# Gated mix of sliding-window attention and a GELU MLP: 256-column products read their moving operand from two halves in turn, and a product and a store stand later in the order

## The chip, the cores and the metric

The kernel runs on one core of one Trainium2 chip. The metric is the device time of one execution in microseconds (us); lower is better. The engines are named as the profile names them: PE does matrix products, PEld the weight loads that overlap them, DVE is the vector engine, ACT the scalar (activation) engine, POOL the third elementwise engine, and SP issues the DMA transfers. Each engine works through its own list of instructions strictly in the order in which the program has them.

## The reference

One sequence of 2048 rows with 512 columns, float32. What is computed, cut to what matters:

```python
def _A_ref(x, wqkv, wo):            # H = 32 heads of 16, window W = 256
    q, k, v = split(x @ wqkv)
    scores = einsum("bhqd,bhkd->bhqk", q, k) * (16 ** -0.5)
    mask = (i - j >= 0) & (i - j < 256)
    p = softmax(where(mask, scores, -1e9))
    return einsum("bhqk,bhkd->bhqd", p, v) @ wo

def _B_ref(x, w1, b1, w2, b2):      # F = 1792
    return gelu(x @ w1 + b1) @ w2 + b2

g = sigmoid((x * gate_w).sum(-1, keepdims=True))
out = g * _A_ref(x, wqkv, wo) + (1 - g) * _B_ref(x, w1, b1, w2, b2)
```

## The kernel before

**Products in three parts.** Every float32 operand of a dense product is split into a high part (rounded to the type that PE multiplies in one pass) and a low part (the rest), and a product is the sum of high x high, high x low and low x high. `mm3` issues these three matmuls. The moving operand (the one that streams through PE, up to 512 columns) can be read straight through or "from its two halves in turn": column 0, column 256, column 1, column 257 and so on. `two` makes that view, and `pairs` is a view of the accumulator with the same order of columns. With both the result lies straight in the accumulator's addresses as streamed, so its reader has to take every second element: `sorted_` gives the first-half columns, then the second-half ones. Before the change, `mm3` does this only for 512 columns.

**Stages.** The 2048 rows are four tiles of T = 512, numbered t = 0 to 3. (1) `qkv(t)` transposes x on PE and makes q, k, v. For t = 0 it begins while the inputs still arrive: the first two q/k products, into accumulators `p[0]` and `p[1]`, are made in column halves of 256 by `qk_half` (48 matmuls, read straight through). `qk_out` then splits each accumulator: ACT copies the high part (`hi`), DVE subtracts the low part (`lo`). (2) Attention runs in 8 groups of 4 heads over 16 key blocks: `att_max` (product `sm`, then a maximum on DVE), `att_exp` (product `st`, exponential on ACT, mask on POOL), `att_pvs` (product with v, once per 512 rows). Its results, numerators and denominators, are added to a tile `nd` on DVE and stored to DRAM as `ND`. (3) Between the attention steps stand the products of the MLP (`mlp`: `u` is the first layer, `gelu` its activation on ACT and DVE, `y` the second layer). (4) `final(t)` loads the normalised attention output `ot` (tiles `ot_0` to `ot_3`, one per 128 columns), splits it into high and low (`hi` on ACT, `lo` on DVE), multiplies by wo into accumulators `a`, and DVE combines with the gate (`ev`, tile `ao`) before the result goes out. There are two accumulators of tag `d`, shared by all dense products. The very last row block is done in two pieces of 256 output columns (LASTN = 2), 24 matmuls, read straight through.

**Normalisation** of the attention output is `att_norm(t, c)`, where t is the row tile and c the quarter of the columns. It works through DRAM: load the denominators into `den`; `rcp` inverts them on DVE; `keep` stores them to `RD`; `back` loads the numerators `num` and the inverses `rb`, the latter spread over 16 rows; `mul` multiplies them on DVE (tile `num`); `store` writes `OT`. `load_part` later reads `OT` into `ot`.

**What sets the order.** The program is written out by a planner with a clock of its own, `now`, in planned nanoseconds. `after(ns, fn)` puts a step on a list with a due time; `tick(ns)` advances the clock by the planned cost of a piece of PE work and writes out all steps that have come due. `fill(ns)` takes dense work until its planned cost is used up, so the attention loop and the dense work are interleaved by planned cost. A `mm3` costs 681 planned ns (MM3), a `qk_half` 119 ns per matmul. DIVS holds the five delays of `att_norm`'s steps (rcp, keep, back, mul, store) from its start: the first row for c = 0 to 2, the second for c = 3. `load_part` asks every 500 planned ns whether its piece of OT is due.

Of the kernel before, what the change touches and what calls it, by code (L numbers as in the profile page):

```python
# [18 lines left out]
T = 512  # L19
NT = S // T  # L20
NB = T // 128
NC = D // 128
# [10 lines left out]
def gated_mix(ctx: ExitStack, tc: tile.TileContext, x, wqkv, wo, w1, b1, w2, b2, gate_w, out):  # L33
# [12 lines left out]
    def f32(ap):  # L46
        return ap.bitcast(F32)
# [60 lines left out]
    def two(v):  # L108

        return v.rearrange("p (a c) -> p c a", a=2)  # L110

    def halves(v):

        return v.rearrange("p (a c) -> p a c", a=2)

    def pairs(p):

        return p.rearrange("p (c a) -> p c a", a=2)
# [3 lines left out]
        return p.rearrange("p (c a) -> p a c", a=2)  # L122

    def mm3(p, lh, ll, rh, rl, first, last):
        if p.shape[1] == T:
            p, rh, rl = pairs(p), two(rh), two(rl)
        nc.tensor.matmul(p, lh, rh, start=first, stop=False)  # L127
        nc.tensor.matmul(p, lh, rl, start=False, stop=False)  # L128
        nc.tensor.matmul(p, ll, rh, start=False, stop=last)  # L129
# [193 lines left out]
    def qk_half(p, j, n, parts):  # L323

        w, xt = wt["qk", j], xts[0]
        h = slice(n * T // 2, (n + 1) * T // 2)
        for a, b in parts:
            for c in range(NC):
                nc.tensor.matmul(p[:, h], w[:, a, c], xt[:, c, b, h], start=(a, b, c) == (0, 0, 0),
                                 stop=(a, b, c) == (1, 0, NC - 1))  # L330
        return len(parts) * NC * 119

    def qk_out(t, j, p):

        i = j % NC
        dst = (SQ, SK)[j // NC][t][i // 2]
        e = sb.tile([128, 2, T], F32R, tag="h", bufs=7, name=f"qke{t}_{j}")

        h = 1 if j < NC else 0

        def hi():
            nc.scalar.activation(halves(e[:, h]), p, AF.Copy)  # L342

        def lo():
            nc.vector.tensor_sub(halves(e[:, 1 - h]), p, halves(f32(e[:, h])))  # L345

        def store():
            to = dst[:, :, :, i % 2].rearrange("h d s c -> (h d) s c")
            nc.sync.dma_start(to[:, 0:2], f32(e))
            if i < 2:  # L350
                nc.sync.dma_start(to[:, 2], f32(e[:, h]))
            else:
                twice.append((t, j, to[:, 2], to[:, h]))
            done.add(("qk", t, j))
        after(100, hi), after(700, lo), after(700 + HOLDQ, store)
# [37 lines left out]
    def qkv(t):  # L393
        last = t == NT - 1
        qk = [("qk", j) for i in range(NC) for j in (i, i + NC)]
        vs = [("v", b) for b in range(NB)]
        pieces = qk[:4] + vs + qk[4:] if last else qk + vs
        if t == 0:
            keys = qk + [("v", c) for c in range(NC)]
            load_xr(0, (0, 1))  # L400
            load_raw(keys[0], True)
            load_xr(0, (2, 3))
            for key in keys[1:]:
                load_raw(key, True)
            nc.sync.dma_start(gwb, gate_w.partition_broadcast(128))
            warm(WARM[0])
            qkv_x(0, 0), qkv_x(0, 1)
            split_now(keys[0], nc.gpsimd.tensor_copy, nc.vector)
            tables()
            warm(WARM[1])  # L410
            p = [ps.tile([128, T], F32, tag="d", bufs=2, name=f"qk0_{n}") for n in range(2)]
            j0, j1 = keys[0][1], keys[1][1]
            yield qk_half(p[0], j0, 0, [(0, 0)])
            qkv_x(0, 2)
            yield qk_half(p[0], j0, 0, [(0, 1), (1, 0)])
            split_now(keys[1], lambda o, i: nc.scalar.activation(o, i, AF.Copy), nc.vector)
            qkv_x(0, 3)
            parts = [(0, 0), (0, 1), (1, 0)]
            yield qk_half(p[1], j1, 0, parts)
            split(keys[2], nc.gpsimd)  # L420
            yield qk_half(p[0], j0, 1, parts)
            qk_out(0, j0, halves(p[0]))
            yield qk_half(p[1], j1, 1, parts)
            qk_out(0, j1, halves(p[1]))
        need(*[("x", t, b) for b in range(NB)])
        for n, (kind, j) in enumerate(pieces):
            if not last and XAT <= n < XAT + NC:
                nc.sync.dma_start(XT[t][n - XAT], f32(xts[t][:, n - XAT]))
            if kind == "qk":
                need(("w", (kind, j)))  # L430
            else:
                need(*[("w", ("v", c)) for c in range(NC)])
            if t == 0 and n == 10:
                nc.sync.dma_start(b1c, b1.rearrange("(f p) -> p f", p=128))
            if t == 0 and n < 2:
                pass
            elif kind == "qk":
                yield from qkv_qk(t, j)
            else:
                yield from qkv_v(t, j)  # L440
            if t == 1 and n % 3 == 2:
                clear_k(n // 3)
            if t == 2 and n < 4:
                clear_q(n)
            if t == 2 and n in (1, 2):
                load_kd(0, n - 1)
            if t == 2 and n in (8, 9):
                load_qd(0, n - 8)
            if t == 0:
                for i in ([3], [4], [5], [6], [7], [8], [9, 10], [11])[n] if n < 8 else []:  # L450
                    split(keys[i], nc.vector if i % 2 else nc.gpsimd)
                if n == 1:
                    after(4000, gate, 0)
                    after(4000, load_xr, 1)
            elif n == 0 and not last:
                load_xr(t + 1)
            if last and n not in (6, 7):
                load(later.pop(0))
            if last and n == len(pieces) - 1:
                for _ in range(4):  # L460
                    load(later.pop(0))
            xat = (5, 7, 8, 9) if t == 0 else (4, 6, 8, 10)
            if not last and n in xat:
                qkv_x(t + 1, xat.index(n))
            if not last and n == xat[-1] + 1:
                gate(t + 1)
# [422 lines left out]
    def final(t):  # L889
        if t == 0:  # L890
            load_o(1)
        ot = xts["o", t]
        parts = {}

        def begin(b, k, n):

            if b == 2 and t < 2:
                load_o(t + 2, range(NC - t))
            if b == 1 and t == 2:
                load_o(NT - 1, range(NC - 1, NC))  # L900
            if k == 0:
                parts[b] = half_pt(f"ao{t * NB + b}")
                after(0, scale_y, t * NB + b, parts[b])
            parts[b, k] = ps.tile([128, D // n], F32, tag="d", bufs=2, name=f"a{t}_{b}_{k}")

        def end(b, k, cs):
            nb, a, p = t * NB + b, parts[b], parts[b, k]

            def ev():
                need(("yb", nb))  # L910
                v = halves(a[:, cs])
                nc.vector.scalar_tensor_tensor(v, (sorted_ if p.shape[1] == T else halves)(p), g[:, nb:nb + 1], v,
                                               op0=ALU.mult, op1=ALU.add)

            def store():
                nc.sync.dma_start(out[nb * 128:(nb + 1) * 128, cs], a[:, cs])
            after(100, ev), after(100 + (HOLDO if nb < NT * NB - 2 else 800), store)

        turns = [(b, c) for b in range(NB) for c in range(NC)]
        if t == NT - 1:  # L920
            turns[:2 * NC] = [(b, c) for h in (range(NC - 1), [NC - 1]) for b in (0, 1) for c in h]
        for b, c in turns:
            n = LASTN if t * NB + b == NT * NB - 1 else 1
            for k in range(n):
                if n > 1:
                    if c:
                        continue
                    row = range(NC)
                else:
                    row = [c]  # L930
                cs = slice(k * D // n, (k + 1) * D // n)
                if c == 0:
                    begin(b, k, n)
                for e in row:
                    need(("w", ("wo", e)), ("ot", t, e))
                    w, ts = wt["wo", e], slice(b * 128, (b + 1) * 128)
                    mm3(parts[b, k], ot[e][:, 0, ts], ot[e][:, 1, ts], w[:, 0, cs], w[:, 1, cs], e == 0, e == NC - 1)
                    yield MM3 / n
                if row[-1] == NC - 1:
                    end(b, k, cs)  # L940
# [105 lines left out]
HOLD = 4000.0  # L1046
HOLDQ = 1500.0
HOLDO = 3000.0
DIVS = ((8000, 10000, 16000, 23000, 25000), (4500, 5700, 8500, 17000, 18500))
REST = 1000.0  # L1050
MXAT = 5500.0
AHEAD = 9e3
# [27 lines left out]
```

## Time and profile before

| | us |
|---|---|
| median of 3 runs | 713.68 (712.69 to 714.38) |
| the profiled execution | 713.22 |
| its span, first to last instruction | 711.4 |
| around the span (difference) | 1.82 |

Busy time and share of the span are given for each engine at the head of the profile; PE's matmuls are pipelined and overlap one another, so its busy time says where it had nothing at all to do, not how fast it went. How fast it went is read from the distance between the starts of neighbouring matmuls in the timeline. The "waits" view lists who waited for whom with the total, the number of times and the longest; the "chain" is the work that ended last, followed back from the end; "windows" gives the busy time of each engine in a stretch of the span. The granted TensorE clock was 1.00 through the run. The groups of instructions that cost most, by engine:

| engine | busiest group | busy us | instructions |
|---|---|---|---|
| PE | `sm` and `st` products of the attention | 295.8 | 1024 |
| DVE | maximum over the scores (`sm`, L555) | 232.8 | 512 |
| POOL | mask of the exponentials (`pt`, L611) | 215.1 | 538 |
| ACT | exponential (`pt`, L617) | 195.4 | 512 |

### The profile page before, as it was taken

How to read it: one execution, taken by the hardware profiler on the slowest of the kernel's cores; microseconds unless marked ns; L12 is line 12 of the kernel's file. 1: busy time of each engine (PE TensorE's matmuls, PEld its weight loads, DVE VectorE, ACT ScalarE, POOL GpSimd, SP SyncE). 2: the span in 40 equal slices, each digit the busy share in tenths (PEclk: the TensorE clock that was granted, in tenths of full speed). 3: DMA queues.
4: the chain of work that ended last, by engine and by line, in shares of the span. 5: the costliest groups of instructions: out<-in, count | busy, mean ns of one | idle time of the engine just before them, and what ended most of it. 6: DMA issues, size and time to landing. Idle time of an engine off the chain costs nothing.

```text
span 711.4 us, 17481 instructions
## 1 busy us (share of the span) xinstructions
PE 694.0 (98%) x6129; PEld 596.5 (84%) x6129; DVE 511.6 (72%) x1561; ACT 419.6 (59%) x972; POOL 365.2 (51%) x852
## 2 busy tenths in 40 slices
PE   9999999998999999999999999999999999999988
PEld 7888888886888888888888877888888888868876
DVE  4632425798769967986898799678968886875552
ACT  4434533378448845864795488458746853885451
POOL 5200001559756866776687578757865875620000
PEclk9999999999999999999999999999999999999999
DMA  9989798999996899999886989997899899477573
GB/s 315 355 256 364 261 373 279 266 295 246 245 249 155 211 274 249 217 279 277 220 194 176 240 234 247 252 260 174 185 246 239 194 260 270 124 217 230 188 243 119
DMA packets 179256, 172.09 MB, mean 242 GB/s; under 512 B 56673, under 2 KB 122977, under 8 KB 179169
## 3 DMA queue, kind: packets, MB, share of 16 engines
q1 hardware_dynamic: 179168, 170.97, 87.4%
q8 instruction: 49, 0.80, 0.5%
q14 instruction: 39, 0.31, 0.2%
HBM read 112.73 MB, written 62.39 MB: 246 GB/s over the span
## 4 chain that ended last, share of the span: by engine, by line
PE 77%; DVE 8%; ACT 5%; DMA 5%; POOL 3%; issue 1%; SPq 0%; DVEq 0%; ACTq 0%; POOLq 0%
PE sm L551 8%; PE pv_sm L639 7%; PE st L595 7%; PE y L127 6%; PE y L129 6%; PE y L128 6%; PE u L127 4%; PE qk L127 4%; PE u L129 4%; PE qk L129 4%; PE u L128 4%; PE qk L128 4%; DVE sm L555 3%; PE v L127 2%; PE v L129 2%; PE v L128 2%
## 5 line engine op out<-in xcount | busy, mean ns | idle before, releaser
L555 DVE CUSTOM_DVE_ANT_1 sm<-sm,mask 128x320 f32<-128x320 f32 (+4 forms) x512 | 232.8, 485 | 66.9 <-PE sm L551 61.8
L611 POOL TENSOR_SCALAR_AFFINE_SELECT pt<-pt 64x256 f32<-64x256 f32 (+1 forms) x538 | 215.1, 420 | 100.0 <-ACT pt L617 89.3
L617 ACT ACTIVATE pt<-st 128x320 f32<-128x320 f32 (+4 forms) x512 | 195.4, 422 | 116.7 <-PE st L595 115.9
L551 PE MATMUL sm<-kd,qd 96*128 96x320 f32 (+4 forms) x512 | 148.2, 303 | 5.0 <-DVE M L555 4.5
L595 PE MATMUL st<-qs,ks 128*128 128x320 f32 (+4 forms) x512 | 147.6, 299 | 1.1 <-ACT pt L617 1.0
L577 POOL CAST qs<-tt 4x256 fp32r<-4x256 f32 x256 | 121.5, 475 | 47.3 <-DVE tt L570 36.7
L551 PEld LDWEIGHTS sm<-kd,qd 96*128 96x128 f32 x512 | 96.8, 189 | 25.4 <-DVE M L555 11.4
L595 PEld LDWEIGHTS st<-qs,ks 128*128 128x128 f32 x512 | 97.5, 191 | 12.7 <-ACT pt L617 2.7
L127 PE MATMUL y<-w,h 128*128 128x512 f32 x224 | 85.1, 380 | 0.6 <-DVE sqh L756 0.6
L129 PE MATMUL y<-w,h 128*128 128x512 f32 x224 | 84.9, 379 | 0.0
L128 PE MATMUL y<-w,h 128*128 128x512 f32 x224 | 84.8, 379 | 0.0
L127 PE MATMUL u<-mx,w 128*128 128x512 f32 x196 | 77.1, 393 | 0.6 <-DVE sqh L756 0.6
L639 PE MATMUL pv_sm<-pt,vbuf 64*32 64x320 f32 (+4 forms) x1408 | 73.7, 346 | 1.0 <-POOL pt L611 1.0
L129 PE MATMUL u<-mx,w 128*128 128x512 f32 x196 | 74.3, 379 | 0.0
L128 PE MATMUL u<-mx,w 128*128 128x512 f32 x196 | 74.2, 378 | 0.0
L639 PE MATMUL pv_st<-pt,vbuf 64*32 64x320 f32 (+4 forms) x1408 | 73.5, 346 | 0.2 <-POOL pt L611 0.2
L555 DVE DVE_READ_ACCUMULATOR2_ANT M<- 128x1 f32 x512 | 71.5, 140 | 0.0
L639 PEld LDWEIGHTS pv_sm<-pt,vbuf 64*32 64x32 f32 x1408 | 49.3, 106 | 21.5 <-issue 2.0
L345 DVE TENSOR_TENSOR qke<-qk,qke 128x512 fp32r<-128x512 f32 x32 | 22.1, 690 | 43.2 <-ACT qke L342 28.2
L342 ACT ACTIVATE qke<-qk 128x512 fp32r<-128x512 f32 x32 | 19.1, 597 | 51.4 <-PE qk L129 30.0
L129 PEld LDWEIGHTS y<-w,h 128*128 128x128 f32 x224 | 42.2, 189 | 6.1
L660 ACT ACTIVATE nd<-pv_st 128x512 f32<-128x512 f32 x32 | 19.1, 597 | 45.2 <-PE pv_sm L639 39.4
(148 smaller groups left out, 1308.5 us busy)
## 6 DMA issues: line engine op xcount, KB each, us to landing
kd<-SK SPq DMA_DIRECT2D x32, 384.0 KB
qs<-SQ SPq DMA_DIRECT2D x64, 192.0 KB
mx<-XT SPq DMA_DIRECT2D x24, 512.0 KB
SQ<-qke SPq DMA_DIRECT2D x16, 512.0 KB
SK<-qke SPq DMA_DIRECT2D x16, 512.0 KB
ND<-nd SPq DMA_DIRECT2D x32, 256.0 KB
raw_w<-in_B_w_dram SPq DMA_DIRECT2D x28, 256.0 KB
qd<-SQ SPq DMA_DIRECT2D x32, 192.0 KB
```

Of the source, the lines that this page charges most:

```text
L127: nc.tensor.matmul(p, lh, rh, start=first, stop=False)
L128: nc.tensor.matmul(p, lh, rl, start=False, stop=False)
L129: nc.tensor.matmul(p, ll, rh, start=False, stop=last)
L342: nc.scalar.activation(halves(e[:, h]), p, AF.Copy)
L345: nc.vector.tensor_sub(halves(e[:, 1 - h]), p, halves(f32(e[:, h])))
L551: nc.tensor.matmul(v, qd[0:96, n, pr, 128 * j:128 * (j + 1)], two(kd[0:96, n, pr, k1 - w:k1]), start=True, stop=True)
L555: nc.vector.tensor_tensor_reduce(v, v, two(mask[:, 320 - w:320]), 1.0, -3e38, ALU.add, ALU.max, M[:, 2 * (b % RB) + hb, pr:pr + 1])
L577: nc.gpsimd.tensor_copy(dst, src.unsqueeze(1).broadcast_to([4, 2, RB, 32]))
L595: nc.tensor.matmul(pairs(p[:, :w]), ks[:, slot(g_, kb // NB), pr, at:at + 128], two(qs[:, pr, k0:k0 + w]), start=True, stop=True)
L611: nc.gpsimd.affine_select(out=v, in_=v, pattern=[[0, v.shape[1]], [1 - 2 * e, 64]], compare_op=ALU.is_ge, fill=0.0, base=-e, channel_multi ...
L617: nc.scalar.activation(halves(pt[:, hf, pr, :w]), sorted_(p[:, :w]), AF.Exp, scale=SCALE)
L639: nc.tensor.matmul(pv[r // 64][32 * i:32 * i + 32, q - c * T:e - c * T], vts[g_, b // NB][r:r + 64, v:v + 32], rhs(r), start=start, stop=s ...
```

## The change

`mm3` now reads from two halves in turn whatever the width, which concerns the 24 matmuls of 256 columns at the end; the reader of those accumulators (`ev` in `final`) always uses `sorted_`. `qk_half` does the same for its 48 matmuls; its accumulator now holds each half of 256 columns interleaved by itself, so `qk_out` gets a four-dimensional view of it and a matching view (`quarters`) of what it writes and subtracts. The planned cost of such a matmul goes from 119 to 109 ns. In DIVS's first row `mul` goes from 23000 to 24500 and `store` from 25000 to 25700 planned ns.

```diff
     def mm3(p, lh, ll, rh, rl, first, last):
-        if p.shape[1] == T:
-            p, rh, rl = pairs(p), two(rh), two(rl)
+        p, rh, rl = pairs(p), two(rh), two(rl)
...
-                nc.tensor.matmul(p[:, h], w[:, a, c], xt[:, c, b, h], start=(a, b, c) == (0, 0, 0),
+                nc.tensor.matmul(pairs(p[:, h]), w[:, a, c], two(xt[:, c, b, h]), start=(a, b, c) == (0, 0, 0),
                                  stop=(a, b, c) == (1, 0, NC - 1))
-        return len(parts) * NC * 119
-
-    def qk_out(t, j, p):
+        return len(parts) * NC * 109
+
+    def quarters(v):
+
+        return v.rearrange("p (n a c) -> p n a c", n=2, a=2)
+
+    def qk_out(t, j, p, of=halves):
...
-            nc.scalar.activation(halves(e[:, h]), p, AF.Copy)
+            nc.scalar.activation(of(e[:, h]), p, AF.Copy)
...
-            nc.vector.tensor_sub(halves(e[:, 1 - h]), p, halves(f32(e[:, h])))
+            nc.vector.tensor_sub(of(e[:, 1 - h]), p, of(f32(e[:, h])))
...
-            qk_out(0, j0, halves(p[0]))
+            qk_out(0, j0, p[0].rearrange("p (n c a) -> p n a c", n=2, a=2), quarters)
...
-                nc.vector.scalar_tensor_tensor(v, (sorted_ if p.shape[1] == T else halves)(p), g[:, nb:nb + 1], v,
+                nc.vector.scalar_tensor_tensor(v, sorted_(p), g[:, nb:nb + 1], v,
...
-DIVS = ((8000, 10000, 16000, 23000, 25000), (4500, 5700, 8500, 17000, 18500))
+DIVS = ((8000, 10000, 16000, 24500, 25700), (4500, 5700, 8500, 17000, 18500))
```

The planned cost of the first stage falls by 48 x 10 = 480 ns, and that moves the interleaving of dense and attention work in the whole program. On PE, where the attention's first score products (`sm`) enter the q/k products of t = 3, before:

```order
L551 MATMUL sm_0_1_1251<-kd,qd 128x64
L551 MATMUL sm_0_0_1253<-kd,qd 128x64
L127 MATMUL qk_1_1236<-xt_1009,qk_297 128x512
L128 MATMUL qk_1_1236<-xt_1009,qk_297 128x512
L129 MATMUL qk_1_1236<-xt_1009,qk_297 128x512
L127 MATMUL qk_1_1236<-xt_1009,qk_297 128x512
L128 MATMUL qk_1_1236<-xt_1009,qk_297 128x512
L129 MATMUL qk_1_1236<-xt_1009,qk_297 128x512
L551 MATMUL sm_0_3_1265<-kd,qd 128x128
L551 MATMUL sm_0_2_1267<-kd,qd 128x128
```

and in the changed kernel:

```order
L126 MATMUL qk_1_1236<-xt_1009,qk_297 128x512
L127 MATMUL qk_1_1236<-xt_1009,qk_297 128x512
L128 MATMUL qk_1_1236<-xt_1009,qk_297 128x512
L554 MATMUL sm_0_1_1254<-kd,qd 128x64
L554 MATMUL sm_0_0_1256<-kd,qd 128x64
L126 MATMUL qk_1_1236<-xt_1009,qk_297 128x512
L127 MATMUL qk_1_1236<-xt_1009,qk_297 128x512
L128 MATMUL qk_1_1236<-xt_1009,qk_297 128x512
L126 MATMUL qk_5_1266<-xt_1009,qk_328 128x512
L127 MATMUL qk_5_1266<-xt_1009,qk_328 128x512
```

One dense product of three matmuls now stands ahead of the first two score products instead of behind them. From there on, 1633 of the 2392 attention matmuls have one dense product more ahead of them than before, 755 have as many as before, and 4 have two more; at the end of attention the count is equal again, and the order of PE from the first matmul of `final` to the end is the same.

On SP, the transfers at the head of `final`, where the last `nd` (the tile `nd_3`) is stored and its denominators are loaded, before:

```order
L734 DMA ot_3_10057<-OT_104 128x512
L689 DMA num_3_10066<-ND_3_118 128x1x512
L689 DMA rb_3_10068<-RD_3_134 128x1x512
L667 DMA ND_3_122<-nd_3_10052 128x512
L734 DMA ot_0_10083<-OT_105 128x512
L734 DMA ot_1_10085<-OT_105 128x512
L734 DMA ot_2_10087<-OT_105 128x512
L916 DMA out_dram<-ao_9984 128x512
L677 DMA den_3_10106<-ND_3_122 128x1x32
```

and in the changed kernel:

```order
L737 DMA ot_3_10057<-OT_104 128x512
L670 DMA ND_3_122<-nd_3_10052 128x512
L692 DMA num_3_10070<-ND_3_118 128x1x512
L692 DMA rb_3_10072<-RD_3_134 128x1x512
L737 DMA ot_0_10083<-OT_105 128x512
L737 DMA ot_1_10085<-OT_105 128x512
L737 DMA ot_2_10087<-OT_105 128x512
L919 DMA out_dram<-ao_9981 128x512
L680 DMA den_3_10106<-ND_3_122 128x1x32
```

The store of `nd_3` moved ahead of the two loads `num` and `rb` of the row tile before it; the rest is as it was. A little further down the same list, with OT_105 the attention output of row tile t = 2 and OT_106 that of t = 3, before:

```order
L689 DMA num_3_10169<-ND_3_122 128x1x512
L689 DMA rb_3_10171<-RD_3_138 128x1x512
L734 DMA ot_3_10176<-OT_105 128x512
L734 DMA ot_0_10178<-OT_106 128x512
L734 DMA ot_1_10180<-OT_106 128x512
L734 DMA ot_2_10182<-OT_106 128x512
```

and in the changed kernel:

```order
L692 DMA num_3_10169<-ND_3_122 128x1x512
L692 DMA rb_3_10171<-RD_3_138 128x1x512
L737 DMA ot_0_10176<-OT_106 128x512
L737 DMA ot_1_10178<-OT_106 128x512
L737 DMA ot_2_10180<-OT_106 128x512
L737 DMA ot_3_10189<-OT_105 128x512
```

The load of the fourth piece of t = 2 moved from ahead of the first three pieces of t = 3 to behind them. ACT's and DVE's steps on these pieces moved less: the split of `ot_3` now stands behind that of `ot_0`, and ahead of those of `ot_1` and `ot_2`.

On DVE, one of the twelve products `mul` that DIVS's first row places (`num_2` of row tile 3), before:

```order
L663 TENSOR_TENSOR nd_0_8418<-nd_0_8418,pv_0_sm 128x512
L555 ISA sm_1_1_8441,M_0_8338<-sm_1_1_8441,mask 128x192
L555 ISA M_0_8338 128x1
L693 TENSOR_TENSOR num_2_8314<-num_2_8314,rb_2_8316 128x512
L555 ISA sm_1_0_8458,M_0_8338<-sm_1_0_8458,mask 128x192
L555 ISA M_0_8338 128x1
L768 TENSOR_TENSOR h_10_8324<-x1h_10_8324_8330,h_10_8324 128x512
```

and in the changed kernel:

```order
L558 ISA sm_1_3_8475,M_0_8343<-sm_1_3_8475,mask 128x256
L558 ISA M_0_8343 128x1
L684 RECIPROCAL den_2_8321<-den_2_8321 128x32
L696 TENSOR_TENSOR num_2_8323<-num_2_8323,rb_2_8325 128x512
L558 ISA sm_1_2_8486,M_0_8343<-sm_1_2_8486,mask 128x256
L558 ISA M_0_8343 128x1
```

Two more maxima (`sm_1_0` and `sm_1_3`) now stand ahead of the product, and with them the inversion `den_2` of the next row tile, which stood behind it.

More of the change, by code (lines that the diff above doesn't have):

```diff
@@ L421, in qkv @@
             yield qk_half(p[0], j0, 1, parts)
-            qk_out(0, j0, halves(p[0]))
+            qk_out(0, j0, p[0].rearrange("p (n c a) -> p n a c", n=2, a=2), quarters)
             yield qk_half(p[1], j1, 1, parts)
-            qk_out(0, j1, halves(p[1]))
+            qk_out(0, j1, p[1].rearrange("p (n c a) -> p n a c", n=2, a=2), quarters)
         need(*[("x", t, b) for b in range(NB)])
```

## Prediction, made before the changed kernel ran

> **What bounds the kernel now.** I began with the head of the page, then took the windows of three stretches (start in us, length, then busy time of each engine) and the waits of PE (total, times, longest).
>
> ```profile
> span 711.4 us, 17481 instructions
> 0.00:142.00 142.00, 140.47 (x713) 122.95 (x714) 66.89 (x177) 58.46 (x145) 26.79 (x65) 1.00 0.91 308
> 142.00:660.00 518.00, 507.97 (x5116) 434.79 (x5115) 420.85 (x1348) 343.18 (x797) 338.44 (x788) 1.00 0.90 229
> 660.00:711.40 51.40, 45.57 (x304) 38.71 (x303) 23.82 (x39) 17.94 (x32) 0.00 (x0) 0.99 0.56 186
> PE sm L551 <- DVE M L555: 4.5, 10, 1.0
> PE a L127 <- DVE ao L912: 2.6, 2, 2.4
> ```
>
> PE (the first busy time) is busy for 140.5 of 142 us, then 508 of 518, then 45.6 of 51.4. So PE sets the end, and a saving counts where PE itself works or waits. The attention stretch loses ten waits for DVE; `final` loses nearly everything in one wait for `ao`.
>
> **The reading from two halves.** These are rows of the timeline: start, length, engine, line.
>
> ```profile
> 704.29 0.38 PE L129 MATMUL a<-wo,ot 128*128 128x512 f32 x1
> 704.50 0.38 PE L127 MATMUL a<-wo,ot 128*128 128x512 f32 x1
> 705.15 0.28 PE L127 MATMUL a<-wo,ot 128*128 128x256 f32 x1
> 705.27 0.28 PE L128 MATMUL a<-wo,ot 128*128 128x256 f32 x1
> 655.86 0.38 PE L595 MATMUL st<-qs,ks 128*128 128x256 f32 x2
> 656.08 0.38 PE L127 MATMUL y<-w,h 128*128 128x512 f32 x1
> ```
>
> Matmuls overlap, so a matmul costs the distance to the next start. 512 columns, read in turn, take 0.21 us. 256 columns, read straight (L127, L128), take 0.12. The two `st` matmuls are 256 columns read in turn, and take 0.22 together, 0.11 each. I take a saving of 10 ns for each of the 72 matmuls, between 0 (the change does nothing) and 14 (half of the 512-column row, 106).
>
> [...]
>
> *At the start* not all 48 matmuls count.
>
> ```profile
> 7.64 0.62 ACT L416 ACTIVATE qk<-raw_qk 128x512 fp32r<-128x512 f32 x1
> 8.32 4.57 PE L329 MATMUL qk<-ks,qk 128*128 128x256 f32 x36
> 11.48 0.60 ACT L342 ACTIVATE qke<-qk 128x512 fp32r<-128x512 f32 x1 [1.83 <-PE qk L329]
> 12.12 0.69 DVE L345 TENSOR_TENSOR qke<-qk,qke 128x512 fp32r<-128x512 f32 x1 [2.25 <-ACT qke L342]
> 12.86 0.19 PEld L127 LDWEIGHTS qk<-ks,qk 128*128 128x128 f32 x1 [0.18 <-DVE qke L345]
> ```
>
> The first twelve are followed by a wait for a weight split (ACT until 8.26, PE at 8.32). Of the 36 after it, the last twelve lie beside the emptying of the first accumulator (ACT 11.48, DVE 12.12 to 12.81), which the next product waits for at 12.86. What is left is 24 x 10 ns = 0.24 us earlier, and the PE wait there grows by the 0.12 that the last twelve save. The emptying itself reads every second element now; other `qke` copies already do so, and the copy here takes the 0.60 that the group of all 32 has as its mean:
>
> ```profile
> L342 ACT ACTIVATE qke<-qk 128x512 fp32r<-128x512 f32 x32 | 19.1, 597 | 51.4 <-PE qk L129 30.0 <-issue 8.6 <-DMA SQ<-qke 6.4
> 708.22 0.48 DVE L912 SCALAR_TENSOR_TENSOR ao<-a,g,ao 128x256 f32<-128x256 f32 x1 [0.88 <-PE a L129]
> ```
>
> *At the end* all 24 lie on the path: the last `ao` (708.22) waits 0.88 for PE and ends the work. That is 24 x 10 ns = 0.24 us. Its reading in turn I cost at nothing.
>
> **The product `mul`, 1500 planned ns later** (twelve times).
>
> ```profile
> DVE num L693 <- DMA rb<-RD: 1.6, 2, 1.3
> 560.34 0.69 DVE L693 TENSOR_TENSOR num<-num,rb 128x512 f32<-128x512 f32 x1 [1.32 <-DMA rb<-RD]
> 561.66 0.30 PE L595 MATMUL st<-qs,ks 128*128 128x320 f32 x1
> 562.56 0.48 PE L127 MATMUL u<-mx,w 128*128 128x512 f32 x1 [0.60 <-DVE sqh L756]
> ```
>
> Twice of twelve DVE stands still until `rb` has landed, 1.6 us in all. The longer time is at 560.34, and there PE is late: `u` starts 0.90 after an `st` that costs 0.14, so 0.76 is lost, waiting for a DVE step queued behind `mul`. With two more maxima ahead (0.4 to 0.5 us each), the landing is covered. I take 0.8 us, between 0 (DVE is still late) and 1.6 (all of DVE's standstill was PE's). `den`'s inversion now comes before `mul`; its data were loaded ahead of `rb`, so it waits for nothing new. The store, 700 later, stands 1200 behind `mul` instead of 2000: SP may wait there for DVE, with loads queued behind that are wanted several us later; I cost that at nothing, up to 0.5 us if such a load is late once.
>
> **The order of transfers in `final`.** First `nd_3`. These are pieces of the chain (start, length), then SP, DVE, PE and ACT.
>
> ```profile
> 667.63 0.60 SPq L689 DMA_DIRECT2D num<-ND  x1
> 669.00 6.65 DMA ND<-nd
> 671.42 0.79 SPq L916 DMA_DIRECT2D out_dram<-ao  x1
> 675.71 2.63 DMA den<-ND
> 678.46 0.35 DVE L681 RECIPROCAL den<-den 128x32 f32<-128x32 f32 x1 [3.99 <-DMA den<-ND]
> 681.27 0.48 PE L127 MATMUL a<-wo,ot 128*128 128x512 f32 x1 [2.41 <-DVE ao L912]
> 676.27 1.87 ACT L737 ACTIVATE ot<-ot 128x512 fp32r<-128x512 f32 x3 [4.88 <-DMA ot<-OT]
> ```
>
> DVE stands at the inversion until `den` lands at 678.34, `ao` stands behind it, and PE waits 2.41 us for that. In the changed order the store goes out where `num` did, at 667.63, ahead of two loads. It lands earlier, and `den` goes out right behind the `out_dram` store, at about 672.2 instead of 675.71. But SP's transfers land in the order of issue: the first `ot`, issued next after ND, is there at 676.27, 0.6 after ND (669.00 + 6.65 = 675.65). Two more `ot` and `out_dram` at 0.6 each make 678.1, and `den`, now directly behind them, lands at about 678.2. What is ahead of it is the same amount in another order. So this wait stays: I take 0, at best the 2.4 us (rival 1).
>
> Then the fourth piece of t = 2, now loaded behind three pieces of t = 3.
>
> ```profile
> 686.71 0.63 ACT L737 ACTIVATE ot<-ot 128x512 fp32r<-128x512 f32 x1 [6.11 <-DMA ot<-OT]
> 688.15 0.63 ACT L737 ACTIVATE ot<-ot 128x512 fp32r<-128x512 f32 x1 [0.81 <-DMA ot<-OT]
> 689.09 1.32 ACT L737 ACTIVATE ot<-ot 128x512 fp32r<-128x512 f32 x2 [0.31 <-DMA ot<-OT]
> 687.49 0.68 DVE L740 TENSOR_TENSOR ot<-ot 128x512 fp32r<-128x512 f32 x1
> 688.50 0.38 PE L127 MATMUL a<-wo,ot 128*128 128x512 f32 x1
> 688.93 0.38 PE L129 MATMUL a<-wo,ot 128*128 128x512 f32 x1
> ```
>
> ACT waits for these four landings: 686.71, 688.15, 689.09 and, the second of the x2, about 689.78. The first is the fourth piece of t = 2; its high part is ready at 687.34, its low part at 688.17, and PE uses them at 688.50 and 688.93. The slack is 0.8 to 1.2 us, and PE has no other dense work there: its order is a plain list, both accumulators are in use, and everything of `final` is queued behind. As the fourth of four it lands at 689.78; ACT copies until 690.41, DVE subtracts until 691.1. The third matmul of the product moves from 688.93 to 691.1, **2.2 us later**, a new wait on PE. All after it moves along, as PE runs without a gap of this size to the end. Bounds: 0 if it lands within the slack, 2.9 if one more transfer (0.7) gets ahead.
>
> **The order elsewhere.** 1633 of 2392 attention matmuls have one dense product (3 x 0.21 us) more ahead. PE's work is the same, only its waits fall otherwise. The ten waits for the maxima (4.5 us) can shrink or grow; I see no reason for a side and take 0, between -1.5 and +1.5, a third of them.
>
> **The sum**, against the profiled execution (713.22 us: span 711.4 and 1.82 around it): -0.24 - 0.24 - 0.8 + 2.2 = +0.92, so **714.1 us**. The median of the three runs, 713.68, is 0.46 above the profiled one, less than the runs differ among themselves (1.69); I leave the forecast at 714.1. A change of 0.2%, 1.43 us, is about what a measurement of this kernel can tell from none: below 712.25 is faster, above 715.11 slower.
>
> **The rivals.**
>
> 1. *`den` lands earlier, and PE's big wait goes.* If a small transfer does not queue behind the others, it lands 2.63 after its issue at 672.2, at 674.9, 3.4 earlier. Then DVE is held by the `ot` pieces only (ACT from 676.27), `ao` comes 2.3 earlier, and the later loads 2.7 earlier too, so the fourth piece lands at 687.1 and its low part is ready at 688.4: PE stands 0.5 better than before instead of 2.2 worse. Sum: 713.22 - 0.24 - 0.24 - 0.8 - 0.5 = 711.4. For it speaks that `den` is only 128 x 32; against it that the three `ot` landed in order.
> 2. *The slower side: a dense product ahead pushes the maxima.* Each extra product brings its DVE steps of 0.68 us (as L740 above) in front of maxima for which PE waits for an accumulator. If half of such a step, 0.34, falls on seven of the ten waits, that is +2.4: 716.5. It decides from 0.14 on each (1.0 in all, past 715.1). Against it speaks that DVE is busy for 421 of 518 us, so it can catch up.
> [...]
>
> **Chances.** Forecast (new wait at the fourth piece) 0.45, own range 712.4 to 715.9; rival 1 0.32; rival 2 0.15; rival 3 0.08. Faster: three quarters of rival 1 and a tenth of the forecast, 0.28. Slower: nearly all of rival 2, a fifth of the forecast, a part of rival 3, together 0.27. Within 0.2%: 0.45. The range goes from 711.2 (just below rival 1) to 716.2 (most of rival 2).
>
> **What would show it.** Right: starts of 256-column matmuls 0.11 apart; no wait of `num` for `rb`; `den` waited for until about 678 (on before's clock) and PE's wait of 2.4 still there; a new PE wait of about 2 us at the third row tile of `final`, ending with ACT's copy and DVE's subtraction of `ot_3`. Wrong: `den` landing within 3 us of its issue; `ot_3` landing before PE gets to it; PE's total of waits between 142 and 660 us off by more than 1.5.

## The result, and the profile after

The changed kernel is **slower by 0.53%**: median 718.88 us (714.25 to 721.18, 22 runs) against 714.14 (712.34 to 718.44, 22 runs), ratio 1.0053, 95% interval 1.0035 to 1.0071, which is 2.5 to 5.1 us. The forecast was 714.1, within 0.2% of before, and the range ended at 716.2. The profiled execution of the changed kernel took 718.97 us.

The head of its page, the windows (start:end, length, then PE, PEld, DVE, ACT, POOL busy; the mean granted clock is the third number from the end) and two of PE's waits:

```profile
span 716.9 us, 17489 instructions
0.00:142.00 142.00, 140.04 (x710) 122.71 (x711) 66.44 (x175) 58.63 (x145) 26.16 (x63) 1.00 0.91 311
142.00:660.00 518.00, 508.97 (x5114) 434.60 (x5113) 420.51 (x1349) 341.94 (x793) 338.36 (x790) 1.00 0.89 227
660.00:716.90 56.90, 48.07 (x308) 40.07 (x306) 24.97 (x41) 18.90 (x35) 0.00 (x0) 0.97 0.56 179
PE sm L554 <- DVE M L558: 2.4, 6, 0.7
PE a L126 <- DVE ao L915: 5.4, 2, 5.2
```

The stretch from 660 us is 56.9 us long instead of 51.4: all 5.5 us by which the span grew. In the attention PE was idle 1.0 us less than before, and the waits for the maxima fell from 4.5 to 2.4. The one large wait, for `ao`, rose from 2.6 to 5.4. The timeline of the changed kernel around it (start, length; the last number is the idle time before):

```profile
679.16 0.38 PE L128 MATMUL a<-wo,ot 128*128 128x512 f32 x1
684.75 0.79 PE L126 MATMUL a<-wo,ot 128*128 128x512 f32 x1 [5.21 <-DVE ao L915]
685.34 0.63 PE L127 MATMUL a<-wo,ot 128*128 128x512 f32 x1
685.76 0.63 PE L128 MATMUL a<-wo,ot 128*128 128x512 f32 x1
687.47 0.53 PE L126 MATMUL a<-wo,ot 128*128 128x512 f32 x1
687.84 0.38 PE L127 MATMUL a<-wo,ot 128*128 128x512 f32 x1
681.94 0.35 DVE L684 RECIPROCAL den<-den 128x32 f32<-128x32 f32 x1 [6.57 <-DMA den<-ND]
682.21 0.63 DVE L696 TENSOR_TENSOR num<-num,rb 128x512 f32<-128x512 f32 x1
682.75 1.28 DVE L743 TENSOR_TENSOR ot<-ot 128x512 fp32r<-128x512 f32 x2
683.95 0.74 DVE L915 SCALAR_TENSOR_TENSOR ao<-a,g,ao 128x512 f32<-128x512 f32 x1
693.16 1.67 ACT L740 ACTIVATE ot<-ot 128x512 fp32r<-128x512 f32 x3 [2.81 <-DMA ot<-OT]
693.84 0.48 PE L126 MATMUL a<-wo,ot 128*128 128x512 f32 x1 [0.23 <-ACT ot L740]
```

Three things are to be seen. DVE stands 6.57 us at the inversion of the last `den`, where it stood 3.99, and `ao` comes four steps behind. After the gap of 5.2 us PE's matmuls start 0.43 us apart instead of 0.216, until 687.5. And the fourth `ot` piece (693.16) is waited for, as forecast, but only briefly. Against the same instructions of before, PE's first product of `final` starts 0.6 us later, the one behind the wait for `ao` 3.5 later (684.75 against 681.27), the next row block 5.0 later, and the first product behind the fourth piece 5.7 later; the last two halves win back 0.2. So 2.9 us are the longer wait, 1.5 the slow matmuls, 0.8 the fourth piece, 0.6 came from earlier. The last is not shown to belong to the change: in the second pair of profiles, further down, the changed kernel reaches `final` earlier than the kernel before (660.1 against 662.4).

Why `den` is late is seen 32 us before it lands. SP's rows, first of the changed kernel, then of the kernel before (loads of other tiles, and rows that nothing here rests on, are left out), and then what SP waited for in the changed kernel between 640 and 662 us:

```profile
642.42 1.15 SPq L670 DMA_DIRECT2D ND<-nd  x1
...
646.72 0.62 SPq L680 DMA_DIRECT2D den<-ND  x1
647.39 1.40 SPq L737 DMA_DIRECT2D ot<-OT  x3
649.69 0.31 SPq L699 DMA_DIRECT2D OT<-num  x1
650.06 0.42 SPq L687 DMA_DIRECT2D RD<-den  x1
654.58 0.32 SPq L737 DMA_DIRECT2D ot<-OT  x1
655.42 0.62 SPq L692 DMA_DIRECT2D num<-ND  x1
657.47 0.60 SPq L670 DMA_DIRECT2D ND<-nd  x1
```

```profile
640.93 1.12 SPq L667 DMA_DIRECT2D ND<-nd  x1
...
645.08 0.62 SPq L677 DMA_DIRECT2D den<-ND  x1
645.85 0.35 SPq L696 DMA_DIRECT2D OT<-num  x1
646.25 1.40 SPq L734 DMA_DIRECT2D ot<-OT  x3
648.16 0.43 SPq L734 DMA_DIRECT2D ot<-OT  x1
653.42 0.61 SPq L689 DMA_DIRECT2D num<-ND  x1
654.82 0.40 SPq L667 DMA_DIRECT2D ND<-nd  x1
```

```profile
SPq L737 <- DMA OT<-num: 4.0, 1, 4.0
```

The store `OT` of row tile t = 0, fourth quarter, used to go out ahead of the three `ot` loads of that tile. The 480 planned ns put it behind them. There it lands 4.9 us after its issue instead of 2.0 (at 654.57, before at 647.89), and SP stands 4.0 us at the fourth `ot` load, which reads what it wrote; `num`, `rb` and the next `ND` are queued behind. Before, SP had no such wait; it stood 2.8 us here for another reason (`vbuf`, for PE), so that only a part of the 4.0 is lost at once.

From here on the normalisations of t = 1, 2 and 3 run one behind another through the same queue, and the delay grows: counted from the issue of t = 1's `ND` store (the first row of each fence), `num` goes out 0.5 us later than before, the next `ND` 1.2 later, and the last `den` lands 2.0 later. I measure this chain from that issue to that landing: 37.4 us in the profile of before, 39.4 in that of the changed kernel. In this pair the chain also starts 1.5 us later in the changed kernel (642.42 against 640.93), so of the 3.5 us by which `den` lands later, 2.0 are the chain's own.

**Theory:** the loss is this order of SP's transfers; the reading in turn and the later division have no part in it. **Rivals:** the reading or the division costs something elsewhere; the denser order in attention costs; the last `ND` store's new place, or the fourth piece alone, sets the end; the slow matmuls come from transfers beside them.

### The profile page after: what moved, and what is told of

It is laid out like the page before. It is cut to its first block, busy times and chain, and to the rows that moved or that the text cites. A ratio compares the mean times of both kernels' runs of the same rounds, so it can differ in the third digit from the quotient of the medians.

```text
span 716.9 us, 17489 instructions
## 1 busy us (share of the span) xinstructions
PE 697.1 (97%) x6129; PEld 597.4 (83%) x6129; DVE 511.9 (71%) x1561; ACT 419.5 (59%) x972; POOL 364.5 (51%) x852
## 4 chain that ended last, share of the span: by engine, by line
PE 74%; DMA 9%; DVE 8%; ACT 5%; issue 2%; SPq 1%; POOL 0%; DVEq 0%; ACTq 0%; POOLq 0%
PE sm L554 8%; PE st L598 7%; PE pv_sm L642 7%; PE y L126 5%; PE y L128 5%; PE y L127 5%; PE u L126 5%; PE u L128 4%; PE u L127 4%; PE qk L126 4%; PE qk L128 4%; PE qk L127 4%; DVE sm L558 2%; DMA ot<-OT 2%; PE v L126 2%
## 5 line engine op out<-in xcount | busy, mean ns | idle before, releaser
L580 POOL CAST qs<-tt 4x256 fp32r<-4x256 f32 x256 | 119.5, 467 | 48.2 <-DVE tt L573 37.6
L345 ACT ACTIVATE qke<-qk 128x512 fp32r<-128x512 f32 x32 | 19.1, 597 | 51.4 <-PE qk L128 29.4
L642 PEld LDWEIGHTS pv_st<-pt,vbuf 64*32 64x32 f32 x1408 | 45.1, 106 | 0.0
```

The source lines that it names most:

```text
L345: nc.scalar.activation(of(e[:, h]), p, AF.Copy)
L580: nc.gpsimd.tensor_copy(dst, src.unsqueeze(1).broadcast_to([4, 2, RB, 32]))
L642: nc.tensor.matmul(pv[r // 64][32 * i:32 * i + 32, q - c * T:e - c * T], vts[g_, b // NB][r:r + 64, v:v + 32], rhs(r), start=start, stop=s ...
```

## The experiments

All ratios are to runs of the kernel before on the same chip; four chips were used, on which its medians were 713.1 to 714.8. Each version has 12 runs where no other number is given.

**The three parts apart.** First the reading alone: the changed kernel with planned cost and DIVS of before, which gives every engine the order of before.

```diff
-        return len(parts) * NC * 109
+        return len(parts) * NC * 119
-DIVS = ((8000, 10000, 16000, 24500, 25700), ...
+DIVS = ((8000, 10000, 16000, 23000, 25000), ...
```

> The reading in turn alone: planned cost of a 256-column product back at 119, division times of before, so every engine's order is that of before. Order theory (the loss comes from where the transfers of final moved): no loss, 48 matmuls on the path at 8 ns less each (median distance 112 ns against 120) = 0.4 us below the kernel before, ratio 0.998 to 1.001, the window from 660 us again 51 us long. Reading theory (the reading itself costs something elsewhere): ratio 1.003 or more.

Measured: 712.36 us, ratio 0.9983 (0.9966 to 1.0000). Next, the planned cost alone, in the kernel before:

```diff
-        return len(parts) * NC * 119
+        return len(parts) * NC * 109
```

> The planned cost 109 alone: matmuls read as before, division times of before; PE's order is that of the changed kernel and SP's order in final too. Order theory: nearly the whole loss is here, 3.5 to 5.5 us over before, ratio 1.004 to 1.008; PE's wait for ao in final over 4.5 us, and matmuls 0.43 us apart after it. Rival (the loss needs the reading or the division): ratio below 1.002, the wait for ao 2.6 us or less.

Measured: 718.30 us (6 runs), ratio 1.0071 (1.0047 to 1.0095). And the division alone, also in the kernel before:

```diff
-DIVS = ((8000, 10000, 16000, 23000, 25000), ...
+DIVS = ((8000, 10000, 16000, 24500, 25700), ...
```

> The division's product and store later, alone; PE's order and SP's order in final are those of before. Order theory: 0 to 0.8 us below before (no wait of num for rb), ratio 0.998 to 1.001, the wait for ao in final 2.6 us. Division theory (the store 1200 behind the product delays OT and all behind it): ratio 1.003 or more, with the wait for ao above 4 us.

Measured: 711.40 us, ratio 0.9968 (0.9947 to 0.9988). PE's wait for `ao` in the three, in this order (the 0.2 of the first is at a later product; where the others wait, PE stands 0.1 us):

```profile
PE a L126 <- DVE ao L915: 0.2, 1, 0.2
PE a L127 <- DVE ao L912: 5.6, 2, 5.4
PE a L127 <- DVE ao L912: 0.7, 2, 0.5
```

So one number in the planner, with no instruction added or changed, carries the whole loss, and the two other parts each come out a little faster, the reading by an interval that just reaches 1.

**Reading and division together, in the order of before** (the changed kernel with 119 for 109):

> Reading in turn and the later division together, planned cost 119, so that PE's order and SP's order in final are those of before. If the two gains add: 0.9983 x 0.9968 = 0.995, 710.2 us. If both come through the same thing (den a little earlier in final): ratio 0.997 to 0.999. Rival (the two together, not the cost, make the loss): over 1.002.

Measured: 711.97 us, ratio 0.9983 (0.9959 to 1.0008). No loss, so the two together are not its cause, but the gains do not add either. In this profile PE waited 3.0 us for `ao`, though it reached `final` at the same time as in the first profile of before (660.64 against 660.63).

**The store put back.** The changed kernel; only `OT` of t = 0 goes ahead of its `ot` loads again:

```diff
-            after(ns, fn)
+            after(ns - (1000 if fn is store and (t, c) == (0, NC - 1) else 0), fn)
```

> The changed kernel with one store planned 1000 earlier: OT of row tile 0, last chunk, goes out ahead of the three ot loads of row tile 0, as before; PE's order unchanged, the other order differences of final (ND ahead of num and rb, the fourth ot piece last) stay. Order theory: the chain of transfers runs 2.5 to 3 us earlier, den of the last division lands near 679 instead of 681.8, PE's wait for ao is 2 to 3 us instead of 5.4 and no matmul after it is 0.43 us apart; then the fourth ot piece costs up to 2.2 us: 714.3 to 716.5, ratio 1.000 to 1.003 to before. Rival (this store has no part in it, den is late from the backlog alone): wait for ao stays over 4.5 us and the ratio over 1.004.

Measured: 715.84 us, ratio 1.0025 (1.0001 to 1.0049), 3.0 us below the changed kernel's median; the chain took 37.8 us. That is about half of the loss (1.0053 before this move), and the two intervals overlap; a cleaner measure of this store follows below. The time is as expected, the wait is not: 3.7 us, with slow matmuls behind it, since PE reached `final` 2.5 us earlier than in the changed kernel's profile:

```profile
PE a L126 <- DVE ao L915: 3.9, 2, 3.7
```

**All three moves of SP in `final` undone**, PE's order still the changed one: also the last `ND` store 400 later, and `OT` of t = 2 600 earlier, which puts the fourth piece first. (A third line, not shown, starts the normalisation behind the `ND` store 400 sooner after it, so that its time stays.)

```diff
-            after(HOLD if g_ * NT + c < NQ - 4 else 800, store)
+            after(HOLD if g_ * NT + c < NQ - 4 else 800 + 400 * (g_ * NT + c == NQ - 1), store)
...
-            after(ns, fn)
+            after(ns - (1000 if t == 0 else 600) * (fn is store and c == NC - 1 and t in (0, 2)), fn)
```

> The changed kernel with three stores moved by 400 to 1000 planned ns, so that SP's order in final (OT of row tile 0 ahead of its ot loads, num and rb ahead of the last ND, fourth ot piece of row tile 2 ahead of the three of row tile 3) is that of before; PE's order stays the changed one, with the dense products earlier in attention. Tail theory (all of the loss is in these transfers): ND(1) issue to den(3) landing 35 to 37.5 us instead of 39.4, PE's wait for ao 2.6 us or less, ratio 0.995 to 1.000. Rival (the order in attention costs too, PE reaching final early is of no use): wait for ao 3.5 us or more, ratio over 1.002.

Measured: 712.33 us, ratio 0.9975 (0.9947 to 1.0004), chain 35.6 us, wait 1.2. This takes the denser order in attention out of the list of suspects: it is still in this kernel. To single out the `ND` store, two of the three moves undone, the `ND` store left as changed:

> The changed kernel with two of the three moves undone (OT of row tile 0 ahead of its ot loads, fourth ot piece first); the last ND store stays ahead of num and rb, the only row in which it differs from the kernel with all three undone (ratio 0.9975). ND theory (with ND early, rb and num land later, den waits behind them and the three ot loads; in the kernel with only OT undone den took 7.1 us from issue to landing): ratio 1.000 to 1.0025, PE's wait for ao 2.5 to 4 us. The forecast's own view (what is ahead of den is the same amount in another order): ratio 0.995 to 0.999, as with all three.

Measured: 712.04 us, ratio 0.9993 (0.9960 to 1.0025), chain 35.5 us. The `ND` store costs nothing that shows, as the forecast had it; the theory given for this run falls. These rows are the wait for `ao` with all three undone, and with two:

```profile
PE a L126 <- DVE ao L915: 1.4, 2, 1.2
PE a L126 <- DVE ao L915: 2.0, 2, 1.9
```

**The fourth piece alone** put first again (the 600 for t = 2 and nothing else):

> The changed kernel with the store of OT of row tile 2 planned 600 earlier, which puts one load back: the fourth ot piece of row tile 2 ahead of the three of row tile 3; everything else as in the changed kernel. In its profile the piece landed at 693.14 as the last of four; as the first it lands 2 to 3 us earlier. If both theories hold (PE is late by its wait for ao and by slow matmuls, and the fourth piece adds 0.4 + 0.2 + 0.1 behind that): 0.6 to 1.2 us less than the changed kernel, ratio 1.003 to 1.005, PE's wait for ao over 4.5 us and matmuls 0.43 us apart still there. Rival (the fourth piece sets the end alone, the wait for ao is hidden behind it): 2 us or more less, ratio under 1.0025.

Measured: 717.60 us, ratio 1.0048 (1.0018 to 1.0078). The loss stays, so the piece does not set the end alone. This kernel and the one with two moves undone differ in SP's list only by `OT` of t = 0, behind its `ot` loads here and ahead of them there: 1.0048 against 0.9993, about 0.55%, with intervals that hardly overlap. This is the cleanest measure of that store. The fourth piece is worth little while the store is late (1.0053 last, 1.0048 first); with the store back it is 1.0025 against 0.9993, about 2.3 us, though there the intervals overlap more.

**The slow matmuls.** First 26 extra matmuls in the changed kernel ahead of the wait, to shorten PE's gap:

```diff
+                if (t, b, c) == (1, 2, 0):
+                    f = ps.tile([128, 320], F32, tag="sm", bufs=3, name="filler")
+                    for _ in range(26):
+                        nc.tensor.matmul(f[:, 0:256], wt["wo", 0][:, 0, 0:128], wt["wo", 0][:, 0, 0:256], start=True, stop=True)
```

> The changed kernel with 26 extra matmuls of 256 columns (about 3.1 us, result unused) on PE just ahead of the product that waits for ao in final, so that PE stands still some 2.3 us there instead of 5.4; nothing else moves. Clock theory (a gap longer than about 3 us makes the next 7 to 13 matmuls take 0.43 us instead of 0.216): matmuls after the wait 0.22 apart, 1.5 to 2.8 us less than the changed kernel, so 716.1 to 717.4, ratio to before 1.001 to 1.004, granted clock 0.999 or 1.0 in most runs instead of 0.992 to 0.998. Rival (the slow matmuls come from transfers or copies beside them, not from the gap): still 0.43 apart, ratio 1.004 or more.

Measured: 718.63 us (4 runs), ratio 1.0075 (1.0049 to 1.0100). A miss that tells nothing apart: `den` came later in this profile, so a gap of 2.99 us was left, the matmuls after it were slow, and the fourth piece was waited for as well (the first row holds 25 of the 26):

```profile
679.73 3.15 PE L938 MATMUL filler<-wo 128*128 128x256 f32 x25
685.88 0.80 PE L126 MATMUL a<-wo,ot 128*128 128x512 f32 x1 [2.99 <-DVE ao L915]
686.47 0.63 PE L127 MATMUL a<-wo,ot 128*128 128x512 f32 x1
```

Then 40 of them, with the fourth piece first:

> The previous kernel with 40 extra matmuls of 256 columns (about 4.8 us, result unused) on PE ahead of the wait for ao, so that PE's gap there is 1 us or less; in the run with 26 of them a gap of 2.99 us was left and the matmuls after it were still 0.43 us apart, and the fourth piece was waited for behind it. Clock theory: no matmul 0.43 apart, granted clock 0.999 or 1.0 in most runs, and now that the fourth piece is there 1.5 to 2.8 us less than the previous kernel, ratio under 1.003. Rival (the slow matmuls come from something else, or cost nothing since another transfer is waited for anyway): no gain, within 0.5 us of the previous kernel.

Measured: 715.22 us, ratio 1.0025 (1.0001 to 1.0049). Here is PE at the wait, without the extra matmuls (two rows of the kernel with the fourth piece first) and with them:

```profile
684.72 0.79 PE L126 MATMUL a<-wo,ot 128*128 128x512 f32 x1 [4.20 <-DVE ao L915]
685.31 0.63 PE L127 MATMUL a<-wo,ot 128*128 128x512 f32 x1
```

```profile
679.06 4.95 PE L938 MATMUL filler<-wo 128*128 128x256 f32 x40
684.24 0.48 PE L126 MATMUL a<-wo,ot 128*128 128x512 f32 x1 [0.23 <-DVE ao L915]
684.56 0.38 PE L127 MATMUL a<-wo,ot 128*128 128x512 f32 x1
```

The same product starts at about the same time, but with PE kept busy it runs at full pace. The granted clock of whole runs says the same: 0.999 or more in 11 of 12 runs with the 40 matmuls, in none of 12 without. So the slow matmuls come from the gap. The medians differ by 2.4 us, as expected, though the two intervals overlap, so that size is less sure than its sign.

**The inversion moved behind `ao` on DVE**, in the changed kernel:

```diff
-            after(ns, fn)
+            after(ns + 2500 * (t == NT - 1 and c == NC - 1 and fn in (rcp, keep)), fn)
```

> The changed kernel with one DVE step moved: the inversion of the last den stands behind the first two ao of row tile 1 in final instead of ahead of them (its store RD moves with it on SP). DVE theory (den holds DVE and ao behind it, that is PE's wait): PE's wait for ao falls from 5.4 us to 3 or less although den lands no earlier, no matmul 0.43 us apart; the pieces of ot are behind it, so 1.5 to 4.5 us less than the changed kernel: 714.4 to 717.4. Rival (ao waits for the ot pieces or for ACT anyway): wait still over 4 us, ratio 1.004 or more.

Measured: 720.27 us (6 runs), ratio 1.0094 (1.0058 to 1.0129). Half a hit: the wait for `ao` fell to 3.0 us as expected, but the time did not fall, since PE then stood at the fourth piece, behind the same late chain:

```profile
PE a L126 <- ACT ot L740: 3.5, 1, 3.5
PE a L126 <- DVE ao L915: 3.2, 2, 3.0
```

The same move where that piece comes first, on the order of before with reading and division:

> Reading in turn, later division, planned cost 119 (order of before), and the inversion of the last den moved on DVE behind the first ao of row tile 1 in final; product mul of the division before is then ahead of it, so OT of row tile 2 is stored up to 3 us earlier. The fourth ot piece is the first of four here, so it should not take over the wait as it did when the same move was made in the changed kernel. DVE theory: PE's wait for ao 1 us or less and no slow matmuls in the profile, 1 to 2.5 us less than without the move (711.97): 709.5 to 711, ratio 0.994 to 0.9975. Rival (ao or the fourth piece waits for transfers anyway): ratio 0.998 or more.

Measured: 712.83 us, ratio 0.9984 (0.9961 to 1.0007). And on the kernel with all three moves undone:

> The changed kernel with SP's order in final as before (three stores moved, 712.33) and the same move of the inversion behind the first ao. DVE theory: 1 to 2.6 us less, 709.7 to 711.3, ratio 0.994 to 0.997, wait for ao 1 us or less, granted clock 0.999 or more in nearly all runs. Rival: within 0.5 us of 712.33.

Measured: 713.61 us, ratio 1.0001 (0.9975 to 1.0026). Two misses: the wait for `ao` at that product went away (the longest left for any `ao` are 0.9 and 0.2 us, at later products), and the time stayed. In the second, PE stood 1.5 us at the fourth piece instead. DVE's order alone is therefore not the bound; that the chain of transfers behind it is fits these 1.5 us, but the first of the two does not show it.

**Both kernels profiled again**, unchanged:

> The kernel before, unchanged, profiled a second time. If its wait for ao is its own: 2 to 3 us again. If it differs between executions as the kernels of the same order suggest: anywhere between 0.2 and 3.4 us, and slow matmuls behind it if it comes to 3 us or more.

Measured: 714.35 us; wait for `ao` 1.8 us, chain 36.8 us.

> The changed kernel, unchanged, profiled a second time. Order theory: OT of row tile 0 issued behind its ot loads and the load behind it blocked until it lands, den landing 39 us or more after the issue of ND(1), wait for ao 4 us or more with matmuls 0.43 us apart behind it. If the first profile was an odd one: a wait of 3 us or less.

Measured: 718.64 us; wait 6.0 us, chain 41.8 us, SP again 4.6 us at the fourth `ot` load:

```profile
PE a L127 <- DVE ao L912: 2.0, 2, 1.8
PE a L126 <- DVE ao L915: 6.1, 2, 6.0
SPq L737 <- DMA OT<-num: 4.6, 1, 4.6
```

So the wait differs by some us between executions of kernels with the same order (0.1 to 3.0), yet the two kernels stay apart.

All seventeen profiles in one table, sorted by where that one store stands. The chain is counted as above, each from one profile:

| `OT` of t = 0 | profiles | chain, us | ratio to before |
|---|---|---|---|
| ahead of its `ot` loads | 10 | 35.1 to 38.0 | 0.9968 to 1.0025 |
| behind them | 7 | 38.5 to 41.8 | 1.0025 to 1.0094 |

The two groups do not overlap in the chain, though the margin is narrow, and four of the ten above have the changed order on PE. In the ratio they meet only at the kernel with the 40 extra matmuls.

## Why the prediction was wrong

- **"The order of transfers in `final`"** began at the fourth `ot` piece of t = 1, and this is the step that failed: "What is ahead of it is the same amount in another order. So this wait stays: I take 0". The amount ahead of `den` was judged rightly; when that queue begins to move was not looked at. The place that decided it is about 20 us earlier on SP, `OT` of t = 0 behind its own `ot` loads. The prediction counted "the order elsewhere" in PE's and DVE's lists only, and took 0 for it. In its place, in two profiles of each kernel: chain 39.4 and 41.8 us instead of 37.4 and 36.8, wait 5.2 and 6.0 us instead of 2.4 and 1.8.
- **The wait was priced by its length alone.** The 5.2 us gap of the first profile cost more than itself: the matmuls behind it started 0.43 us apart instead of 0.216, which came to 1.5 us. Of three gaps of about 3.0 us, two were followed by a lower granted clock and one was not (last section).
- **The last `ND` store, 0:** right. The run in which it alone stayed changed shows no loss, and in the profiles of both kernels `den` landed 0.2 us behind the `out_dram` store issued ahead of it.
- **The fourth piece, +2.2:** right mechanism, wrong size. It is waited for where forecast, with ACT's copy and DVE's subtraction ending the wait, but PE is itself 5 us late there, so only 0.8 us are left in the first profile. When PE came sooner (inversion moved), it was 3.5; and with the store of t = 0 back, the two places of the piece differ by about 2.3 us (their intervals overlap), near the 2.2 that the forecast had.
- **The reading in turn, -0.24 twice:** the mechanism holds. The 36 matmuls at the start took 4.29 us instead of 4.57, 8 ns each, and those at the end start 0.11 us apart:

```profile
9.07 4.29 PE L328 MATMUL qk<-ks,qk 128*128 128x256 f32 x36
712.23 0.28 PE L126 MATMUL a<-wo,ot 128*128 128x256 f32 x1
712.35 0.28 PE L127 MATMUL a<-wo,ot 128*128 128x256 f32 x1
```

  That the reading brings nothing at 256 columns (the third rival, 0.08 in the chances) falls with that: no run shows a cost of it, and what was measured for this operand is a gain. Alone it came to 0.17% (0 to 0.34%).
- **The product `mul`, -0.8:** right side, mechanism not shown. In the changed kernel's first profile no `num` waits for `rb`, but in its second one does, for 1.3 us; with the division alone one waits 0.7, and with the planned cost alone, where the division is that of before, none does. So the wait does not follow the division's delays in these profiles. Alone, the division gave 0.32% (0.12 to 0.53%), 0.9 to 3.8 us, at least the forecast's term; where it gained that stays open.
- **These two gains do not show in the changed kernel.** Time that PE saves ahead of `final` can turn into waiting for the chain there; that is argued, not shown, since PE's arrival at `final` differs by up to 4.8 us between the profiles (657.7 to 662.4).
- **Rival 2, the slower side** (dense products push the maxima), had the sign and not the place: those waits fell. **Rival 1** (`den` lands earlier) had the right place with the wrong sign: `den` went out earlier, but landed 3.5 us later.

Beating both kernels: the division alone, in the order of before, is the only version whose interval lies wholly below 1. Not run, and left open: why the chain differs by some 3 us between profiles with the same order, and why reading and division together gave no more than each alone.

## What to carry to other kernels

When a planner's cost changes, compare the order of every queue, the DMA issuer's first, from where the last chain of transfers starts, not only around the wait that is seen at the end. Look for a store that has slipped behind loads while another load behind it reads what it writes: the issuing engine stands there (SP stood 4.0, 4.1 and 4.6 us in three profiles here), and what is queued behind it pays. Where PE waits at the end for a chain of round trips, work saved ahead of it can turn into waiting, which is argued here, not shown. A wait of about 3 us or more should be priced with the slow matmuls that came behind most of such waits here (1.5 us behind the 5.2 us of the changed kernel's first profile).

## What the runs showed of the hardware

Behind the gap of 5.2 us in the changed kernel's `final`, seven matmuls of 512 columns (684.75 to 687.47) started 0.42 to 0.59 us apart; ahead of the gap it was 0.216. The granted clock was 0.50 there instead of 1.00. In five profiles the longest gap in `final` was 1.2 to 2.4 us, and the granted clock of the profiled execution was 1.000; in six there was one of 3.5 to 6.0 us, and it was 0.995 to 0.998. Of three gaps of about 3.0 us, the one with the 26 extra matmuls (2.99) had matmuls 0.43 us apart behind it; reading and division together (3.00) had a granted clock of 0.997; with the inversion moved behind `ao` in the changed kernel (2.97), the matmuls behind the gap stood 0.21 to 0.32 us apart, as behind the gap of 2.41 us in the trace of before.

What parts the last two, as far as the windows show, is where the gap lies to the steps of the clock. In the changed kernel's trace the clock was 0.50 from 684.35 to 687.76 us, that is for 3.41 us, and 1.00 before and after. In the trace of before it went to 0.50 once, at 710.88 us, behind the last product. Counted from the start of each trace's first clock record (5.10 and 4.32 us), these changes lie at 199, 200 and 207 steps of 3.413 us. These are windows of that length, in order of the changed kernel just behind its gap, of reading and division together (gap of 3.00 us) and of the inversion moved behind `ao` (gap of 2.97 us); the number after the comma is PE's busy time, the third from the end the granted clock:

```profile
684.35:687.76 3.41, 3.01 (x7) 2.47 (x8) 1.61 (x3) 0.00 (x0) 0.00 (x0) 0.50 0.68 207
679.10:682.51 3.41, 0.65 (x3) 0.60 (x4) 3.41 (x7) 1.16 (x2) 0.00 (x0) 1.00 0.47 166
680.85:684.27 3.42, 1.59 (x7) 1.43 (x8) 3.20 (x6) 3.42 (x6) 0.00 (x0) 1.00 0.50 190
```

How long PE was idle within one such window went with the clock of the next. In the changed kernel it was idle for the whole window from 680.94 to 684.35 us, and in the trace of before for 2.7 of the 3.41 us ahead of 710.88; 0.50 followed both. Of the gap of 3.00 us, 2.8 lie in the window shown. Of the gap of 2.97 us, 1.8 lie in the window shown and 1.1 ahead of it; the gap of 2.41 us in the trace of before is parted into 1.3 and 1.1 at such a step, and the clock stays at 1.00. What happens between 1.8 and 2.7 us of idle time these windows do not show.
